# Four tiles for w_in and a new order of batch 0's prologue in a fused cosformer attention and gated MLP kernel

## The chip, the cores and the metric

The kernel runs on one core of a Trainium2 chip. The metric is device time in microseconds (us) of one execution, the median of several. Smaller is better. One further execution is taken by the hardware profiler, and all views of the profile come from it. The engines are called by their short names there: PE (TensorE's products), PEld (its weight loads), DVE (VectorE), ACT (ScalarE), POOL (GpSimd), SP (SyncE, which here only issues loads and stores).

## What is computed

Eight batches, eight heads, 576 positions of 64 numbers each. Linear attention with the feature map phi (a relu times a cosine and a sine of the position, side by side, so 128 features), then a two-layer MLP with x * sigmoid(1.702 x) between.

```python
def phi(x, c, s):
    r = np.maximum(x, 0.0)
    return np.concatenate([r * c, r * s], axis=-1)
q_p = phi(q, cos_w, sin_w)
k_p = phi(k, cos_w, sin_w)
kv = np.einsum('bhsf,bhsd->bhfd', k_p, v)
z = np.sum(k_p, axis=2)
num = np.einsum('bhsf,bhfd->bhsd', q_p, kv)
den = np.einsum('bhsf,bhf->bhs', q_p, z)[..., None] + 1e-06
x = (num / den)                      # then (8, 576, 8 * 64) as 4608 tokens of 512
...
h = x @ w_in                         # 512 x 2048
g = h * (1.0 / (1.0 + np.exp(-1.702 * h)))
return (g @ w_out).astype(np.float32)
```

## The kernel before

The schedule is written out by hand: on each engine the instructions run in the order of the program text, and the framework adds the waits between engines and for loads from what each instruction reads and writes. Matrix operands are bf16, sums are float32 in PSUM. PSUM is used through two pools: `pmm`, four buffers of one bank, and `pat`, two buffers of two banks.

One batch goes through these steps. k and q are loaded as float32 and turned into features by `trig` (line 137), one position block `j` of nine at a time, two instructions each (cosine, sine), on VectorE or, with `act=True`, on ScalarE. One `trig` reads its block for all four pairs of heads. `kv_mm` (L204) multiplies the features of k with v, 36 products of half the array for two pairs of heads; the column of ones beside v gives z. `kv_evac` (L212) copies kv and z to `kvs`. `qturn_pe` (L169) turns two position blocks of q's features with eight transposes on TensorE, and `qevac` (L176) copies them to `qT`. `num_mm` (L218) makes the numerators of one chunk of 128 positions, and in the 65th column of each head the denominators; `num_div` (L226) divides on VectorE: a small add, a reciprocal, and one multiplication of 128x512. `xturn_mm` (L247) transposes the chunk and `xturn_evac` (L254) copies it to x on ScalarE. There are five chunks, the last of 64 positions. `mm1_part` (L271) multiplies x with w_in for one block `fc` of 128 of the 2048 hidden columns, over the four blocks `kc` of the 512; `gelu` (L278) is the activation; `mm2` (L320) multiplies with w_out.

w_in is one tile, `w_in_sb`. `w_in_of(kc, fc)` takes every fourth column of a group of 512, so that `fc // 4` is the group. It is loaded by the Pool queue, which casts to bf16, in three pieces: two groups, then, after a one-element copy that waits for v (`gate`, L133), the other two in one load (L134). A first `gate` (L128) lets v's loads go only after the first piece of k has landed. k and q of batch 0 come by the SP queue, each in two pieces cut along the positions (L61 to L63). Behind w_in the Pool queue issues batch 1's k, two of four w_out groups, batch 1's q and v, and the other w_out groups (L417 to L423), in this order.

Batch 0 has nothing to lie beside, so its prologue is written out at L374 to L414. TensorE is kept busy from the start with products of zeros (`idle`). z of batch 0 is made ahead of v by products with a column of ones, into the same PSUM buffers that later take kv. All of the numerators of chunks 0 and 1 come after both kv groups. Then `start_block` (L345) transposes chunks 0 and 1, makes the numerators of chunk 2, and runs the first four hidden blocks in four pieces of 128 positions, with the numerators and transposes of later chunks between. `mm1(b, 4)` is the first with 512 positions at a time. From there on products follow each other, and the steps of the next batch are placed between them.

Of the kernel before, what the change touches and what calls it, by code (L numbers as in the profile page):

```python
# [9 lines left out]
F32 = mybir.dt.float32  # L10
BF16 = mybir.dt.bfloat16
# [8 lines left out]
def kernel(  # L20
# [39 lines left out]
    qf0 = qf[:, 0:NI * S].rearrange("p (i e) -> p i e", i=NI)  # L60
    for t, src, cut in ((kf, k, 192), (qf0, q, 256)):  # L61
        nc.sync.dma_start(out=t[:, :, 0:cut], in_=src_of(src, 0)[:, :, 0:cut])
        nc.sync.dma_start(out=t[:, :, cut:S], in_=src_of(src, 0)[:, :, cut:S])  # L63


# [32 lines left out]
    qT = one.tile([128, H, 640], BF16, name="qT")  # L98
    w_in_sb = one.tile([128, KC, d_ff], BF16, name="w_in_sb")
    w_out_sb = one.tile([128, FC, d_model], BF16, name="w_out_sb")  # L100
# [5 lines left out]
    wout_r = moe_w_out.rearrange("(g p c) d -> p g c d", p=128, c=4)  # L106
    w_in_v = w_in_sb.rearrange("p k (g f c) -> p k g c f", f=128, c=4)

    def w_in_of(kc, fc):
        return w_in_v[:, kc, fc // 4, fc % 4, :]  # L110

# [8 lines left out]

    def load_win(f0, f1):
        nc.gpsimd.dma_start(out=w_in_sb[:, :, f0:f1], in_=win_r[:, :, f0:f1])  # L122

# [5 lines left out]
    for i in (0, 2):  # L129
        nc.gpsimd.dma_start(out=vb[:, i:i + 2], in_=src_of(v, 0, i, i + 2))  # L130
    load_win(0, 512)
    load_win(512, 1024)
    nc.gpsimd.tensor_copy(gate[0:1, 1:2], vb[0:1, 3, 0:1])  # L133
    load_win(1024, 2048)  # L134

# [59 lines left out]

    def kv_open(i0=0, i1=NI):
        t = pat.tile([128, 2, 512], F32, name="at")
        for i in range(i0, i1):
            st["kv", i] = t[:, :, ds((i - i0) * 65, 65)]
        st["ps", i0] = t[:, :, 0:(i1 - i0) * 65]  # L200
        if i0 == 0:
            st["kvs"] = small.tile([128, 2, NI, VW], BF16, name="kvs", bufs=2)
# [8 lines left out]

    def kv_evac(i0, i1):  # L212
        o = st["kvs"][:, :, i0:i1, 0:65]
        nc.vector.tensor_copy(o, st["ps", i0].rearrange("p hh (i e) -> p hh i e", e=65))  # L214

    nums = {}

    def num_mm(c):  # L218
        ps = pat.tile([128, 2, 512], F32, name="at")
        for h in range(H):  # L220
            i, hh = divmod(h, 2)
            nc.tensor.matmul(ps[:, h // 4, ds((h % 4) * 65, 65)], qT[:, h, ts(c, 128)],  # L222
                             st["kvs"][:, hh, i, 0:65], start=True, stop=True)
        nums[c] = [ps]

    def num_div(c):  # L226
# [43 lines left out]

    def mm1_part(b, fc, t0, t1):  # L271
        if t0 == 0:
            hp[fc] = pmm.tile([128, MT], F32, name="mm")
        for kc in range(KC):
            nc.tensor.matmul(hp[fc][:, t0:t1], w_in_of(kc, fc), x[b][:, kc, t0:t1],  # L275
                             start=(kc == 0), stop=(kc == KC - 1))
# [56 lines left out]

    def idle(n, cols=512):
        w = pmm.tile([128, 512], F32, name="mm")
        for _ in range(n):
            nc.tensor.matmul(w[:, 0:cols], warm[:, 0:128], warm[:, 0:cols], start=True, stop=True)  # L337
# [6 lines left out]

    def start_block(b, opened=False):  # L345

        if not opened:
            xturn_mm(0)
            xturn_evac(b, 0)
            xturn_mm(1)  # L350
            xturn_evac(b, 1)
            num_mm(2)
            num_div(2)
        for c in range(4):
            for fc in range(4):
                mm1_part(b, fc, c * 128, c * 128 + 128)
            if c == 0:
                num_mm(3)
                num_div(3)
                xturn_mm(2)  # L360
                xturn_evac(b, 2)
            if c == 1:
                num_mm(4)
                num_div(4)
                xturn_mm(3)
                xturn_evac(b, 3)
        for fc in range(4):
            gelu(fc)
        mm1(b, 4)
        xturn_mm(4)  # L370
        xturn_evac(b, 4)


    idle(12)  # L374
    idle(100, 64)
    for j in (0, 1):
        trig(kr, kf, j)
    for j in (2, 6, 7, 8):
        trig(kr, kf, j, act=True)
    for j in (3, 4, 5):  # L380
        trig(kr, kf, j)
    kv_open(0, 2)
    kv_open(2, 4)
    kv_mm(0, NI, lambda r, i, j: ones[r, 0:1], 64, 1)
    for j in (0, 1):
        trig(qn0, qf0, j)
    qturn_pe(0)
    for j in (2, 3):
        trig(qn0, qf0, j, act=True)
    qturn_pe(1)  # L390
    idle(3)
    for j in (4, 5):
        trig(qn0, qf0, j)
    qturn_pe(2)
    for j in (6, 7):
        trig(qn0, qf0, j, act=True)
    qevac(0)
    trig(qn0, qf0, 8)
    qevac(1, act=True)
    qevac(2, act=True)  # L400
    kv_mm(0, 2, vb_rhs, 0, 64)
    kv_evac(0, 2)
    kv_mm(2, 4, vb_rhs, 0, 64)
    kv_evac(2, 4)
    qturn_pe(3)
    qevac(3, act=True)
    num_mm(0)
    num_div(0)
    num_mm(1)
    num_div(1)  # L410
    qturn_pe(4)
    qevac(4)
    x_open(0)
    start_block(0)  # L414


# [62 lines left out]
    mm2(0, 3, 12, 16)  # L479
    start_block(1, opened=True)  # L480

# [79 lines left out]
```

## Time and profile before

| | us |
|---|---|
| median of 3 runs | 302.92 (302.34 to 303.1) |
| profiled execution | 303.1 |
| its span, first to last instruction | 301.4 |
| PE busy | 287.0 (95%) |
| PEld busy | 164.4 (55%) |
| DVE busy | 125.9 (42%) |
| ACT busy | 131.4 (44%) |
| POOL busy | 33.9 (11%) |
| mean granted clock of TensorE | 0.989 of full |

In lists of instructions a row has its start and its length in us, the engine, the line, the operation, what it writes and reads, its shape, and how many like it follow (x16); in brackets stands how long the engine was idle before it and what ended that. Rows of loads end with the size in KB and the time from issue to landing. In the chain of waits each piece has its start, its length and what ran. A busy PE is not PE at its peak, since products are pipelined and their ends are modelled.

### The profile page before, as it was taken

The numbers are of one execution on the slowest core, as the hardware profiler recorded it, in microseconds if no ns is written. First come the engines' busy times: TensorE is split into PE (matmuls) and PEld (weight loads), VectorE is DVE, ScalarE is ACT, GpSimd is POOL, SyncE is SP. The second block draws the span as 40 slices with busy tenths as digits, with TensorE's granted clock in tenths as the row PEclk, the third lists the DMA queues.
The fourth block names the chain that finished last, engine by engine and source line by source line (L and its number), as shares of the span: only waits on it lengthen the run. The fifth ranks groups of instructions, "written<-read, shape, count | busy, mean of one in ns | idle before, by whom it ended". The sixth has DMA issues, their size and how long they took to land.

```text
span 301.4 us, 6250 instructions
## 1 busy us (share of the span) xinstructions
PE 287.0 (95%) x2552; PEld 164.4 (55%) x2587; DVE 125.9 (42%) x362; ACT 131.4 (44%) x230; POOL 33.9 (11%) x67
## 2 busy tenths in 40 slices
PE   8829999999999999999999999999999999999995
PEld 4719565685754555455545554555455545565444
DVE  4644802479037444744474447444744430000000
ACT  7822775367311661166116611661166116674111
POOL 6240003240023100100010001000100010000000
PEclk9996999999999999999999999999999999999999
DMA  7999934859536995599549955996599141000331
GB/s 255 235 240 287 344 67 157 310 152 153 159 70 124 362 213 167 107 365 199 179 104 367 193 186 104 366 179 200 102 368 167 54 116 49 3 0 0 80 97 70
DMA packets 66700, 52.38 MB, mean 174 GB/s; under 512 B 47376, under 2 KB 56336, under 8 KB 66672
## 3 DMA queue, kind: packets, MB, share of 16 engines
q1 hardware_dynamic: 59824, 32.52, 42.0%
q0 software_dynamic: 6848, 19.47, 22.4%
q8 instruction: 20, 0.33, 0.4%
q14 instruction: 8, 0.07, 0.1%
HBM read 36.70 MB, written 9.44 MB: 153 GB/s over the span
## 4 chain that ended last, share of the span: by engine, by line
PE 89%; DMA 4%; issue 3%; ACT 1%; POOL 1%; ACTq 0%; POOLq 0%
PE mm L325 41%; PE mm L275 36%; PE mm L293 3%; DMA w_in_sb<-in_moe_w_in_dram 3%; PE at L222 3%; PE at L209 3%; PE mm L302 2%; ACT g L280 1%; DMA kf<-in_k_dram 1%; PE at L252 1%; PE at L173 1%; POOL vb L130 1%; POOL w_in_sb L122 1%; ACT ysb L329 0%; POOL gate L128 0%
## 5 line engine op out<-in xcount | busy, mean ns | idle before, releaser
L275 PE MATMUL mm<-xT,w_in_sb 128*128 128x512 bf16 (+1 forms) x598 | 114.7, 350 | 5.3 <-DMA w_in_sb<-in_moe_w_in_dram 4.9
L325 PE MATMUL mm<-w_out_sb,g 128*128 128x512 bf16 (+1 forms) x506 | 116.3, 373 | 1.3 <-issue 0.2
L275 PEld LDWEIGHTS <-w_in_sb 128*128 128x128 bf16 x608 | 63.6, 115 | 53.9 <-issue 5.0
L280 ACT ACTIVATE g<-mm 128x512 bf16<-128x512 f32 x128 | 75.6, 598 | 32.1 <-PE mm L275 32.1
L325 PEld LDWEIGHTS <-g 128*128 128x128 bf16 x528 | 48.6, 97 | 49.6
L329 ACT ACTIVATE ysb<-mm 128x512 f32<-128x512 f32 (+1 forms) x37 | 21.7, 586 | 111.4 <-PE mm L325 111.4
L332 POOL DMA_DIRECT2D out_dram<-ysb x38 | 20.6, 546 | 177.3 <-ACT ysb L329 177.2
L144 DVE TENSOR_SCALAR kr<-kf,cosw 128x256 bf16<-128x256 f32 x68 | 23.7, 348 | 22.7 <-DMA kf<-in_k_dram 22.7
L234 DVE TENSOR_TENSOR xn<-at,inv 128x512 bf16<-128x512 f32 x40 | 27.6, 691 | 1.6 <-DVE inv L232 0.2
L230 DVE TENSOR_SCALAR den<-at 128x8 f32<-128x8 f32 x40 | 6.6, 166 | 43.9 <-PE at L222 43.9
L144 DVE TENSOR_SCALAR kr<-kf,sinw 128x256 bf16<-128x256 f32 x68 | 23.9, 351 | 0.0
L214 DVE CAST kvs<-at 128x520 bf16<-128x520 f32 (+1 forms) x9 | 5.8, 642 | 33.1 <-PE at L209 33.0
L222 PEld LDWEIGHTS <-qT 128*128 128x128 bf16 x320 | 15.0, 99 | 7.3
L222 PE MATMUL at<-kvs,qT 128*128 128x65 bf16 x320 | 16.4, 196 | 0.0
L157 DVE TENSOR_SCALAR qn<-qf,sinw 128x512 bf16<-128x512 f32 (+1 forms) x30 | 14.3, 477 | 0.0
L157 DVE TENSOR_SCALAR qn<-qf,cosw 128x512 bf16<-128x512 f32 (+1 forms) x30 | 14.3, 476 | 0.0
L209 PEld LDWEIGHTS <-kr 64*128 64x128 bf16 x648 | 10.2, 94 | 3.9 <-issue 3.6
L259 ACT ACTIVATE xT<-at 128x512 bf16<-128x512 bf16 (+1 forms) x10 | 5.6, 563 | 12.2 <-DVE inv L232 9.2
L293 PE MATMUL mm<-xt,w_in_sb 128*128 128x384 bf16 x64 | 10.6, 326 | 0.0
L325 PE MATMUL mm<-w_out_sb,gl_t 128*128 128x512 bf16 x47 | 10.5, 379 | 0.1
L337 PE MATMUL mm<-warm 128*128 128x64 bf16 (+1 forms) x114 | 8.1, 234 | 1.3 <-DVE warm L76 1.3
L293 PEld LDWEIGHTS <-w_in_sb 128*128 128x128 bf16 x64 | 7.2, 113 | 3.3
(60 smaller groups left out, 125.0 us busy)
## 6 DMA issues: line engine op xcount, KB each, us to landing
kf<-in_k_dram SPq DMA_DIRECT2D x5, 1152.0 KB, 6.6
vf<-in_v_dram SPq DMA_DIRECT2D x5, 1152.0 KB, 9.5
qf<-in_q_dram SPq DMA_DIRECT2D x5, 1024.0 KB, 5.5
out_dram<-ysb POOLq DMA_DIRECT2D x20, 256.0 KB, 2.6
kf<-in_k_dram POOLq DMA_DIRECT2D x2, 1152.0 KB, 11.1
vf<-in_v_dram POOLq DMA_DIRECT2D x2, 1152.0 KB, 15.1
out_dram<-ysb POOLq DMA_DIRECT2D x18, 128.0 KB, 3.3
w_out_sb<-in_moe_w_out_dram POOLq DMA_DIRECT2D x4, 512.0 KB, 19.2
```

Source lines behind the costliest of these rows:

```text
L144: nc.vector.tensor_scalar(o, i, 0.0, w[:, j:j + 1], op0=MAX, op1=MUL)
L157: nc.vector.tensor_scalar(o, i, 0.0, sc, op0=MAX, op1=MUL)
L209: nc.tensor.matmul(st["kv", i][:, hh, ds(col, n)], kr[r, j, i, :], rhs(r, i, j), start=(j == 0), stop=(j == NS - 1))
L222: nc.tensor.matmul(ps[:, h // 4, ds((h % 4) * 65, 65)], qT[:, h, ts(c, 128)], st["kvs"][:, hh, i, 0:65], start=True, stop=True)
L234: nc.vector.tensor_tensor(xn, pv[:, :, :, 0:64], inv.unsqueeze(3).to_broadcast([128, 2, 4, 64]), op=MUL)
L275: nc.tensor.matmul(hp[fc][:, t0:t1], w_in_of(kc, fc), x[b][:, kc, t0:t1], start=(kc == 0), stop=(kc == KC - 1))
L280: nc.scalar.activation(g, hp.pop(fc), AF.Gelu_apprx_sigmoid)
L293: nc.tensor.matmul(hps, w_in_of(kc, fc), xt[:, kc, :], start=(kc == 0), stop=(kc == KC - 1))
L325: nc.tensor.matmul(yp[t, c0][:, c0:c1], w, w_out_sb[:, fc, c0:c1], start=(fc == 0), stop=(fc == FC - 1))
L329: nc.scalar.activation(ysb[:, c0:c1], yp[t, c0][:, c0:c1], AF.Identity)
L332: eng.dma_start(out=dst[:, c0:c1], in_=ysb[p0:p0 + n, c0:c1])
L337: nc.tensor.matmul(w[:, 0:cols], warm[:, 0:128], warm[:, 0:cols], start=True, stop=True)
```

## The change

w_in becomes four tiles, one for each group of 512 columns, each with a load of its own. In batch 0's prologue, k is loaded in two pieces cut by pairs of heads and q in one piece, so that each run in memory is whole (576 numbers). z is made by `z_early` in a PSUM buffer of its own and copied to `kvs` at once. The denominators of chunks 0 and 1 are made by `den_mm` (eight products of one column into the buffer of the idle products) and inverted by `den_inv`, `den_mm(w, 0)` ahead of the first kv group, `den_mm(w, 1)` behind it. kv's buffers have 64 columns for each pair, without the one for z. Chunks 0 and 1 are then made by halves of four heads: `num_half`, `div_half`, `turn_half`, `xevac_half`. The q features, turns and evacuations are spread in another order over VectorE and ScalarE, the products of the first two hidden blocks with chunk 0 are split by `kc`, and batch 0's start block is written out with the numerators of chunks 2 to 4 elsewhere. `start_block` is left for batch 1, unchanged there.

```diff
@@ -58,10 +58,9 @@
     qf = one.tile([128, 2560], F32, name="qf")
     kf, vf, vb = raw("kf"), raw("vf"), raw("vb", BF16)
     qf0 = qf[:, 0:NI * S].rearrange("p (i e) -> p i e", i=NI)
-    for t, src, cut in ((kf, k, 192), (qf0, q, 256)):
-        nc.sync.dma_start(out=t[:, :, 0:cut], in_=src_of(src, 0)[:, :, 0:cut])
-        nc.sync.dma_start(out=t[:, :, cut:S], in_=src_of(src, 0)[:, :, cut:S])
-
+    for i in (0, 2):
+        nc.sync.dma_start(out=kf[:, i:i + 2], in_=src_of(k, 0, i, i + 2))
+    nc.sync.dma_start(out=qf0, in_=src_of(q, 0))
 
     NP = NS + 5
     pos_i = const.tile([128, NP], mybir.dt.int32)
@@ -96,7 +95,7 @@
     qn0 = qn.rearrange("p c h f -> p (c h f)")[:, 0:NS * NI * 128].rearrange(
         "p (j i f) -> p j i f", j=NS, i=NI)
     qT = one.tile([128, H, 640], BF16, name="qT")
-    w_in_sb = one.tile([128, KC, d_ff], BF16, name="w_in_sb")
+    w_in_sb = [one.tile([128, KC, 512], BF16, name=f"w_in{g}") for g in range(4)]
     w_out_sb = one.tile([128, FC, d_model], BF16, name="w_out_sb")
     nc.gpsimd.memset(vt[:, :, :, 64:66], 1.0)
     nc.gpsimd.memset(qT[:, :, S:640], 0.0)
@@ -104,10 +103,10 @@
 
     win_r = moe_w_in.rearrange("(kc p) f -> p kc f", p=128)
     wout_r = moe_w_out.rearrange("(g p c) d -> p g c d", p=128, c=4)
-    w_in_v = w_in_sb.rearrange("p k (g f c) -> p k g c f", f=128, c=4)
+    w_in_v = [t.rearrange("p k (f c) -> p k c f", c=4) for t in w_in_sb]
 
     def w_in_of(kc, fc):
-        return w_in_v[:, kc, fc // 4, fc % 4, :]
+        return w_in_v[fc // 4][:, kc, fc % 4, :]
 
     def load(t, src, b, eng=nc.gpsimd):
         eng.dma_start(out=t, in_=src_of(src, b))
@@ -118,8 +117,8 @@
         eng.dma_start(out=qf[0:64, 2048:2560].rearrange("p (h e) -> p h e", h=H),
                             in_=q[b, :, 512:S, :].rearrange("h p d -> p h d"))
 
-    def load_win(f0, f1):
-        nc.gpsimd.dma_start(out=w_in_sb[:, :, f0:f1], in_=win_r[:, :, f0:f1])
+    def load_win(g):
+        nc.gpsimd.dma_start(out=w_in_sb[g], in_=win_r[:, :, ts(g, 512)])
 
     def load_wout(g):
         nc.gpsimd.dma_start(out=w_out_sb[:, ts(g, 4), :], in_=wout_r[:, g])
@@ -128,10 +127,11 @@
     nc.gpsimd.tensor_copy(gate[0:1, 0:1], kf[0:1, 0, 0:1])
     for i in (0, 2):
         nc.gpsimd.dma_start(out=vb[:, i:i + 2], in_=src_of(v, 0, i, i + 2))
-    load_win(0, 512)
-    load_win(512, 1024)
+    load_win(0)
+    load_win(1)
     nc.gpsimd.tensor_copy(gate[0:1, 1:2], vb[0:1, 3, 0:1])
-    load_win(1024, 2048)
+    load_win(2)
+    load_win(3)
 
 
     def trig(dst, src, j, act=False):
@@ -193,12 +193,12 @@
 
     st = {}
 
-    def kv_open(i0=0, i1=NI):
+    def kv_open(i0=0, i1=NI, n=65):
         t = pat.tile([128, 2, 512], F32, name="at")
         for i in range(i0, i1):
-            st["kv", i] = t[:, :, ds((i - i0) * 65, 65)]
-        st["ps", i0] = t[:, :, 0:(i1 - i0) * 65]
-        if i0 == 0:
+            st["kv", i] = t[:, :, ds((i - i0) * n, n)]
+        st["ps", i0] = t[:, :, 0:(i1 - i0) * n]
+        if i0 == 0 and n == 65:
             st["kvs"] = small.tile([128, 2, NI, VW], BF16, name="kvs", bufs=2)
 
     def kv_mm(i0, i1, rhs, col, n):
@@ -209,9 +209,32 @@
                     nc.tensor.matmul(st["kv", i][:, hh, ds(col, n)], kr[r, j, i, :], rhs(r, i, j),
                                      start=(j == 0), stop=(j == NS - 1))
 
-    def kv_evac(i0, i1):
-        o = st["kvs"][:, :, i0:i1, 0:65]
-        nc.vector.tensor_copy(o, st["ps", i0].rearrange("p hh (i e) -> p hh i e", e=65))
+    def kv_evac(i0, i1, n=65):
+        o = st["kvs"][:, :, i0:i1, 0:n]
+        nc.vector.tensor_copy(o, st["ps", i0].rearrange("p hh (i e) -> p hh i e", e=n))
+
+    def z_early():
+        st["kvs"] = small.tile([128, 2, NI, VW], BF16, name="kvs", bufs=2)
+        t = pat.tile([128, 2, 512], F32, name="at")
+        for i in range(NI):
+            for j in range(NS):
+                for hh in range(2):
+                    r = slice(hh * 64, hh * 64 + 64)
+                    nc.tensor.matmul(t[:, hh, i:i + 1], kr[r, j, i, :], ones[r, 0:1],
+                                     start=(j == 0), stop=(j == NS - 1))
+        nc.vector.tensor_copy(st["kvs"][:, :, :, 64], t[:, :, 0:NI])
+
+    def den_mm(dt, c):
+        for h in range(H):
+            i, hh = divmod(h, 2)
+            nc.tensor.matmul(dt[:, ds(c * H + h, 1)], qT[:, h, ts(c, 128)],
+                             st["kvs"][:, hh, i, 64:65], start=True, stop=True)
+
+    def den_inv(dt, c):
+        den = small.tile([128, 2, 4], F32, name="den")
+        nc.vector.tensor_scalar(den, dt[:, ts(c, H)].rearrange("p (a h) -> p a h", a=2), 1e-6, None, op0=ADD)
+        st["inv", c] = small.tile([128, 2, 4], F32, name="inv0", bufs=2)
+        nc.vector.reciprocal(st["inv", c], den)
 
     nums = {}
 
@@ -222,6 +245,31 @@
             nc.tensor.matmul(ps[:, h // 4, ds((h % 4) * 65, 65)], qT[:, h, ts(c, 128)],
                              st["kvs"][:, hh, i, 0:65], start=True, stop=True)
         nums[c] = [ps]
+
+    def num_half(c, a):
+        if a == 0:
+            nums[c] = [pat.tile([128, 2, 512], F32, name="at"),
+                       small.tile([128, 2, 4, 64], BF16, name="xn", bufs=4)]
+        for h in range(4 * a, 4 * a + 4):
+            i, hh = divmod(h, 2)
+            nc.tensor.matmul(nums[c][0][:, a, ds((h % 4) * 65, 64)], qT[:, h, ts(c, 128)],
+                             st["kvs"][:, hh, i, 0:64], start=True, stop=True)
+
+    def div_half(c, a):
+        ps, xn = nums[c]
+        nc.vector.tensor_tensor(xn[:, a], ps[:, a, 0:260].rearrange("p (h e) -> p h e", h=4)[:, :, 0:64],
+                                st["inv", c][:, a].unsqueeze(2).to_broadcast([128, 4, 64]), op=MUL)
+
+    def turn_half(c, a):
+        ps, xn = nums[c]
+        xv = xn[:, a].rearrange("p h e -> p (h e)")
+        for k2 in range(2):
+            nc.tensor.transpose(ps[:, a, ds(264 + k2 * 64, 64)].bitcast(BF16), xv[:, ts(k2, 128)], ident)
+
+    def xevac_half(b, c, a):
+        ps = nums[c][0]
+        i = ps[:, a, 264:392].bitcast(BF16).rearrange("p (k t) -> p k t", k=2)
+        nc.scalar.activation(x[b][:, 2 * a:2 * a + 2, c * 128:c * 128 + 128], i, AF.Copy)
 
     def num_div(c):
         ps = nums[c][0]
@@ -268,10 +316,10 @@
     gT = {}
     hp = {}
 
-    def mm1_part(b, fc, t0, t1):
-        if t0 == 0:
+    def mm1_part(b, fc, t0, t1, k0=0, k1=KC):
+        if t0 == 0 and k0 == 0:
             hp[fc] = pmm.tile([128, MT], F32, name="mm")
-        for kc in range(KC):
+        for kc in range(k0, k1):
             nc.tensor.matmul(hp[fc][:, t0:t1], w_in_of(kc, fc), x[b][:, kc, t0:t1],
                              start=(kc == 0), stop=(kc == KC - 1))
 
@@ -331,8 +379,8 @@
                 eng = nc.sync if b == B - 1 else nc.gpsimd
                 eng.dma_start(out=dst[:, c0:c1], in_=ysb[p0:p0 + n, c0:c1])
 
-    def idle(n, cols=512):
-        w = pmm.tile([128, 512], F32, name="mm")
+    def idle(n, cols=512, w=None):
+        w = pmm.tile([128, 512], F32, name="mm") if w is None else w
         for _ in range(n):
             nc.tensor.matmul(w[:, 0:cols], warm[:, 0:128], warm[:, 0:cols], start=True, stop=True)
 
@@ -342,15 +390,7 @@
     def vt_rhs(r, i, j):
         return vt[r, j, i, 0:65]
 
-    def start_block(b, opened=False):
-
-        if not opened:
-            xturn_mm(0)
-            xturn_evac(b, 0)
-            xturn_mm(1)
-            xturn_evac(b, 1)
-            num_mm(2)
-            num_div(2)
+    def start_block(b):
         for c in range(4):
             for fc in range(4):
                 mm1_part(b, fc, c * 128, c * 128 + 128)
@@ -371,47 +411,88 @@
         xturn_evac(b, 4)
 
 
-    idle(12)
-    idle(100, 64)
-    for j in (0, 1):
+    w = pmm.tile([128, 512], F32, name="mm")
+    idle(12, 512, w)
+    idle(100, 64, w)
+    for j in range(6):
         trig(kr, kf, j)
-    for j in (2, 6, 7, 8):
+    for j in (6, 7, 8):
         trig(kr, kf, j, act=True)
-    for j in (3, 4, 5):
-        trig(kr, kf, j)
-    kv_open(0, 2)
-    kv_open(2, 4)
-    kv_mm(0, NI, lambda r, i, j: ones[r, 0:1], 64, 1)
-    for j in (0, 1):
-        trig(qn0, qf0, j)
+    z_early()
+    trig(qn0, qf0, 0)
+    trig(qn0, qf0, 1, act=True)
+    trig(qn0, qf0, 2)
+    trig(qn0, qf0, 3, act=True)
     qturn_pe(0)
-    for j in (2, 3):
-        trig(qn0, qf0, j, act=True)
+    qevac(0)
+    trig(qn0, qf0, 4)
+    trig(qn0, qf0, 5, act=True)
     qturn_pe(1)
-    idle(3)
-    for j in (4, 5):
-        trig(qn0, qf0, j)
+    qevac(1, act=True)
+    den_mm(w, 0)
+    den_inv(w, 0)
+    kv_open(0, 2, 64)
+    kv_mm(0, 2, vb_rhs, 0, 64)
+    kv_evac(0, 2, 64)
+    den_mm(w, 1)
+    den_inv(w, 1)
     qturn_pe(2)
-    for j in (6, 7):
-        trig(qn0, qf0, j, act=True)
-    qevac(0)
+    qevac(2, act=True)
+    kv_open(2, 4, 64)
+    num_half(0, 0)
+    div_half(0, 0)
+    trig(qn0, qf0, 6)
+    kv_mm(2, 4, vb_rhs, 0, 64)
+    kv_evac(2, 4, 64)
+    turn_half(0, 0)
+    x_open(0)
+    xevac_half(0, 0, 0)
+    num_half(0, 1)
+    div_half(0, 1)
+    num_half(1, 0)
+    div_half(1, 0)
+    trig(qn0, qf0, 7, act=True)
+    num_half(1, 1)
+    div_half(1, 1)
     trig(qn0, qf0, 8)
-    qevac(1, act=True)
-    qevac(2, act=True)
-    kv_mm(0, 2, vb_rhs, 0, 64)
-    kv_evac(0, 2)
-    kv_mm(2, 4, vb_rhs, 0, 64)
-    kv_evac(2, 4)
     qturn_pe(3)
-    qevac(3, act=True)
-    num_mm(0)
-    num_div(0)
-    num_mm(1)
-    num_div(1)
     qturn_pe(4)
+    for fc in (0, 1):
+        mm1_part(0, fc, 0, 128, 0, 2)
+    turn_half(0, 1)
+    xevac_half(0, 0, 1)
+    nums.pop(0)
+    qevac(3)
     qevac(4)
-    x_open(0)
-    start_block(0)
+    turn_half(1, 0)
+    turn_half(1, 1)
+    xevac_half(0, 1, 0)
+    xevac_half(0, 1, 1)
+    nums.pop(1)
+    for fc in (0, 1):
+        mm1_part(0, fc, 0, 128, 2, 4)
+    num_mm(2)
+    num_div(2)
+    for fc in (2, 3):
+        mm1_part(0, fc, 0, 128)
+    num_mm(3)
+    num_div(3)
+    for fc in range(4):
+        mm1_part(0, fc, 128, 256)
+    xturn_mm(2)
+    xturn_evac(0, 2)
+    num_mm(4)
+    num_div(4)
+    xturn_mm(3)
+    xturn_evac(0, 3)
+    for c in (2, 3):
+        for fc in range(4):
+            mm1_part(0, fc, c * 128, c * 128 + 128)
+    for fc in range(4):
+        gelu(fc)
+    mm1(0, 4)
+    xturn_mm(4)
+    xturn_evac(0, 4)
 
 
     load(kf, k, 1)
@@ -477,7 +558,7 @@
     num_mm(2)
     num_div(2)
     mm2(0, 3, 12, 16)
-    start_block(1, opened=True)
+    start_block(1)
 
 
     for b in range(1, B):
```

## The prediction

> **What bounds the kernel now.** I read the page first: TensorE is busy for 95% of a span of 301.4 us, and of the five waits that the list of its waits holds one is long, 4.9 us, for a weight load. Then the chain of waits between 13 and 31 us, and TensorE's instructions in order of time.
>
> ```profile
> 13.35 9.64 DMA w_in_sb<-in_moe_w_in_dram
> ...
> 30.31 0.38 PE mm L275
> ```
> ```profile
> 13.43 1.07 PE L209 MATMUL at<-vb,kr 64*128 64x64 bf16 x60 [1.43 <-issue]
> 14.42 0.62 PE L173 MATMUL mm<-ident,qn 128*128 128x128 bf16 x8
> 14.88 0.66 PE L222 MATMUL at<-kvs,qT 128*128 128x65 bf16 x16
> 15.37 0.39 PE L173 MATMUL mm<-ident,qn 128*128 128x128 bf16 x4
> ...
> 18.03 0.23 PE L275 MATMUL mm<-xT,w_in_sb 128*128 128x128 bf16 x1
> 23.13 1.76 PE L275 MATMUL mm<-xT,w_in_sb 128*128 128x128 bf16 x15 [4.88 <-DMA w_in_sb<-in_moe_w_in_dram]
> ```
>
> The reader should see one product of L275 run at 18.03, and the second wait until 23.13. What it waits for is the third w_in load, issued at 13.35 and landed at 22.99, which brings columns 1024 to 2047; the product needs columns below 512. Of all the data that L275 names, nothing else lands then. So the wait is a false one: with the weights in one tile, its strided slice (every fourth column, `kc` = 1) is taken to overlap the rows that this load writes, while the slice of `kc` = 0 lies below all of them and passed. The stall has a second price, in tables of stages (stage, its length, then busy time of each engine, the granted clock, DMA share, GB/s):
>
> ```profile
> 4.00:6.00 2.00, 2.00 (x23) 1.04 (x22) 1.30 (x4) 0.93 (x3) 1.84 (x4) 1.00 1.07 391
> ...
> 16.00:18.25 2.25, 1.10 (x17) 0.79 (x17) 1.77 (x6) 0.97 (x3) 2.02 (x3) 1.00 1.17 213
> 18.25:23.10 4.85, 0.01 (x1) 0.00 (x0) 1.04 (x3) 0.33 (x1) 0.55 (x1) 0.86 1.10 278
> 23.10:28.30 5.20, 5.17 (x57) 5.20 (x58) 1.38 (x5) 0.60 (x1) 0.00 (x0) 0.50 1.06 268
> ```
>
> After the empty stage TensorE runs for 5.2 us at half clock. The DMA share stays above 1 throughout: the loads go at the rate of the engines, whatever their order.
>
> **What the split of w_in removes.** The first products then need only the first quarter and x. The rows of the loads:
>
> ```profile
> 1.32 0.49 SPq L63 DMA_DIRECT2D kf<-in_k_dram  x1
> 2.40 0.51 SPq L63 DMA_DIRECT2D qf<-in_q_dram  x1
> 4.28 1.63 POOL L130 DMA_DIRECT2D vb<-in_v_dram  x2
> 5.88 1.59 POOL L122 DMA_DIRECT2D w_in_sb<-in_moe_w_in_dram  x2
> ```
> ```profile
> kf<-in_k_dram SPq DMA_DIRECT2D x1, 768.0 KB, 4.7
> qf<-in_q_dram SPq DMA_DIRECT2D x1, 640.0 KB, 7.5
> vb<-in_v_dram POOLq DMA_DIRECT2D x1, 288.0 KB, 8.0
> w_in_sb<-in_moe_w_in_dram POOLq DMA_DIRECT2D x1, 512.0 KB, 9.5
> ```
>
> Issue plus landing: k complete at 6.0, q at 9.9, the second half of v at 5.1 + 8.0 = 13.1, the first quarter of w_in at 15.4. The last is earlier than x (evacuated at 16.95 + 0.60 = 17.6, row below), so the 4.88 us go. The second term is the slow clock. From 23.13 to 30.31 lie 63 products of L275 with 128 columns, 16 of L222 and 8 transposes of L252. At full clock a 128-column product takes 0.058 (eight transposes from 14.42 to 14.88) and one of L222 0.031 (sixteen from 14.88 to 15.37): 71 x 0.058 + 16 x 0.031 = 4.6 us instead of 7.18. Had L275 simply gone on at 18.03, `mm1(0, 4)`, the product at 30.31, would start near 18.03 + 0.06 + 4.6 + 0.1 for a buffer = 22.8: 7.5 us earlier. That is the ceiling.
>
> **What the new prologue gives back.** I walk its order by hand up to the same product. Durations, with start to start where rows follow each other:
>
> ```profile
> 6.07 0.35 DVE L144 TENSOR_SCALAR kr<-kf,cosw 128x256 bf16<-128x256 f32 x1 [0.56 <-DMA kf<-in_k_dram]
> 7.77 0.34 DVE L144 TENSOR_SCALAR kr<-kf,sinw 128x256 bf16<-128x256 f32 x1
> 10.97 0.68 DVE L183 COPY qT<-mm 128x1024 bf16<-128x1024 bf16 x1
> 11.57 0.34 DVE L144 TENSOR_SCALAR qn<-qf,cosw 128x256 bf16<-128x256 f32 x1
> 14.00 0.96 DVE L214 CAST kvs<-at 128x260 bf16<-128x260 f32 x2 [1.82 <-PE at L209]
> 15.33 0.17 DVE L230 TENSOR_SCALAR den<-at 128x8 f32<-128x8 f32 x1 [0.37 <-PE at L222]
> 15.77 0.69 DVE L234 TENSOR_TENSOR xn<-at,inv 128x512 bf16<-128x512 f32 x1
> 28.99 0.34 DVE L144 TENSOR_SCALAR kr<-kf,cosw 128x256 bf16<-128x256 f32 x1
> 33.45 0.34 DVE L144 TENSOR_SCALAR kr<-kf,sinw 128x256 bf16<-128x256 f32 x1
> ```
> ```profile
> 8.48 0.49 ACT L142 ACTIVATE qn<-qf,cosw 128x256 bf16<-128x256 f32 x1
> 11.28 0.49 ACT L142 ACTIVATE qn<-qf,sinw 128x256 bf16<-128x256 f32 x1
> 11.68 1.91 ACT L181 ACTIVATE qT<-mm 128x1024 bf16<-128x1024 bf16 x2
> 16.95 0.60 ACT L259 ACTIVATE xT<-at 128x512 bf16<-128x512 bf16 x1 [0.85 <-PE at L252]
> 32.06 0.43 ACT L259 ACTIVATE xT<-at 128x256 bf16<-128x256 bf16 x1
> ```
>
> A phi on VectorE takes 0.26 (17 steps from 28.99 to 33.45), 0.34 while the Pool queue issues loads (5 steps from 6.07 to 7.77); on ScalarE 0.40 (7 steps from 8.48). A q turn's evacuation takes 0.60 on VectorE, 0.95 on ScalarE; a kv evacuation 0.48; a pair for the denominators 0.44 (15.33 to 15.77). Half a division, 128x256, shows nowhere: between half of 0.69 and all of it; I take 0.35, as 0.69 is nearly all per element. Of products with one column no row is shown: they cost between 0.0165 (half-array products of L209, 60 from 13.43 to 14.42) and 0.031; I take 0.0165 for z, whose weights have the same shape, and 0.031 for the denominators, whose weights are those of L222. A step from one engine to the next I put at 0.15.
>
> k has to be there whole, since each phi reads all of it: the start moves from 4.2 to 6.0. VectorE then does 12 phis, six at 0.34 and six at 0.26: 9.6. Of the 72 z products the first ten go ahead; the others wait for the last phi and end at 10.7. VectorE holds its queue for their copy (0.17 like the row at 15.33), so the first q phi starts at 10.85, later than q's 9.9. From there VectorE's order is nearly gapless: two q blocks to 11.9, evacuation of turn 0 to 12.6, q 4 to 13.1, denominators 13.6, kv of heads 0 to 3 to 14.3 (its products end at 13.8, behind the instruction wait that ended at 13.43 before), denominators 14.75, half division 15.15, q 6 15.7, kv of heads 4 to 7 16.15, three half divisions 17.55, q 8 18.1. ScalarE's share (q 1, 3, 5, 7, turns 1 and 2) lies beside it, and v is early for both kv groups: its gate now waits for 576 KB of k and not 384, 0.2 MB or 0.5 us at 391 GB/s, so its second half lands at 13.6 at worst, and the second group starts at 14.65. TensorE has `qturn_pe(4)` in front of the first products, so these start at 18.35, 0.3 behind the old 18.03.
>
> Behind that: turn 4 0.23, 64 products 3.71, six half-chunk transposes 0.35, 24 number products 0.75, eight transposes 0.46: 5.5 us. Two waits stand in it. The products for `kc` 2 and 3 wait for the second half of chunk 0 (its transposes end at 18.7, its evacuation of 0.43 at 19.3): 0.35. `num_mm(4)` wants the buffer that chunk 2's evacuation of 0.60 frees, and nothing is ahead of it to cover this: 0.77. With 0.4 for semaphores and for the buffer of the first gelu, `mm1(0, 4)` starts at 18.1 + 5.5 + 0.35 + 0.77 + 0.4 = 25.1. **Sum: 30.31 - 25.1 = 5.2 us earlier**, 2.3 short of the ceiling. One more Pool issue (0.8 us) and the wait of batch 1's q load for the last q phi (18.1 instead of 12.2) delay issues behind loads that keep the engines full, so I cost both at nothing. The cover gone, 0.8 would come late where the slack is:
>
> ```profile
> 18.25 0.55 POOL L125 DMA_DIRECT2D w_out_sb<-in_moe_w_out_dram  x1 [0.23 <-DMA w_in_sb<-in_moe_w_in_dram]
> w_out_sb<-in_moe_w_out_dram POOLq DMA_DIRECT2D x1, 512.0 KB, 23.8
> 57.26 1.89 PE L325 MATMUL mm<-w_out_sb,g 128*128 128x512 bf16 x8
> ```
>
> The last load of this stream lands at 42.0, its first reader runs at 57.26, after the change at 52. So the 5.2 us should reach the end. The profiled execution took 303.1 us around its span of 301.4: 303.1 - 5.2 = 297.9. The median shown, 302.92, is 0.2 lower, so I forecast **297.7** for a median. The unknown costs (half divisions up to 0.69 each, column products, semaphores, whole runs landing 0.4 earlier by their longer rows) make it 296.7 to 299.0.
>
> **The rivals.** (a) *Nothing is given back*: k and q land so much earlier in whole runs that the chain hides: 302.9 - 7.5 = 295.4. Against it: the phis of k alone hold VectorE 1.5 us longer than before. 9%. (b) *q comes later*: one long q load shares the engines evenly with v from 5.5 on. Some 1.2 MB of q then take 2.4 MB of traffic, which at 391 GB/s last until 11.6; VectorE's first q phis move by 0.75, ScalarE's by 1.7, turn 0 and all behind it by about 1.1: 298.8. 13%. (c) *The issue of v waits for VectorE's run of phis.* v's second issue, due to start at 5.6, would end with the phis of k at 9.6, land 8.0 later at 17.6, and hold the second kv group from 14.8 to 17.7: +2.9, 300.6. Against it: the two issues beside phis took 1.63, no more than 0.82 each. 5%. [...] (d) *The wait stays*, bound to the load queue and not to the tile: first products again at 23.1, 302.9. Against it: the product at 18.03 passed with the same load in flight. 4%. (e) *The clock falls in the thin prologue* and stays at half for the first 5.2 us of products, as it did from 23.1: 2.6, and TensorE's own pieces of the chain (a q turn 0.46, a denominator group 0.25, a kv group 0.6, number products 0.12) take twice as long, 1.4: 301.7. Against it: 1.10 busy of 2.25 us left it at 1.00, and the longest gap in my walk is about 1 us. 3%. [...] (f) *Slower*: the prologue is now one chain of some 16 steps between engines up to `mm1(0, 4)`, and each costs the 0.85 that ScalarE idled before the evacuation at 16.95, not my 0.15: 16 x 0.7 = 11.2 back, 308.9. It decides from 5.2 / 16 + 0.15 = 0.48 a step. Against it: that 0.85 holds the transposes themselves, and VectorE's 0.37 at 15.33 holds 0.25 of products. 4%.
>
> **How the numbers follow.** The forecast has 62%. A difference under 0.3%, 0.9 us, can't be told from none here. The range from 295.3 to 300.2 holds the forecast, (a) and (b), and leaves (c) to (f) out, 16%, with some of the forecast's tail. Faster: forecast, (a), (b), (c) and most of (e), 0.91; same: (d) and the rest, 0.05; slower: (f), 0.04.
>
> **What would show it.** Right: no wait of L275 for w_in, clock 1.00 throughout 18 to 30 us, the first q phi near 10.85, the first 128-column product near 18.4, the first 512-column product near 25.1, everything later shifted alike. The forecast falls if the first product waits for q, v or a load, if a stage ahead of 25 us shows a clock under 1, or if the distance gained at 25 us shrinks again before the end.

## The result and the profile after

| us | before | after |
|---|---|---|
| median of 13 runs | 302.65 (302.09 to 303.42) | 301.06 (299.11 to 302.07) |
| profiled execution | 303.1 | 300.57 |
| its span | 301.4 | 298.9 |
| mean granted clock in it | 0.989 | 0.983 |

The ratio is 0.9943, 95% interval 0.9923 to 0.9963: faster, by 1.7 us and not by the 5.2 of the forecast. Of the 13 executions after, two took 299.1 us with a mean clock of 0.994, the others 300.6 to 302.1 with 0.977 or 0.983. One execution of `mended` below (310.75 us) fell in a slower state of the chip and is left out of its median and ratio.

The wait for w_in is gone; the list of TensorE's waits no longer names a load. In its place the table by stages of the kernel after (start:end, length, busy time of PE, PEld, DVE, ACT, POOL with counts, granted clock, DMA share, GB/s) shows:

```profile
8.00:10.00 2.00, 1.59 (x69) 1.38 (x67) 1.55 (x6) 0.60 (x3) 0.00 (x0) 1.00 1.14 231
10.00:12.00 2.00, 1.21 (x55) 1.05 (x48) 1.23 (x6) 2.00 (x6) 0.00 (x0) 0.99 1.19 199
12.00:14.00 2.00, 1.96 (x44) 1.59 (x44) 1.51 (x5) 1.36 (x2) 0.57 (x2) 0.50 1.24 204
...
20.00:22.00 2.00, 1.81 (x17) 1.51 (x15) 1.38 (x4) 0.30 (x1) 1.07 (x2) 0.50 1.23 227
22.00:24.00 2.00, 1.96 (x42) 1.87 (x41) 1.11 (x4) 0.74 (x3) 1.55 (x3) 0.94 1.07 403
```

The half clock has not gone, it has moved: it was at 21.7 to 28.6 us and is now at 12.0 to 22.2, over most of the chain that leads to the first products. The chain of waits of the kernel after:

```profile
5.94 3.62 DVE kr L144 x12
9.56 0.04 issue
9.61 0.95 PE at L223 x62
10.58 0.19 DVE kvs L225
10.77 0.51 DVE qn L144 x2
11.28 0.05 issue
11.33 1.48 PE mm L173 x16
...
27.71 0.38 PE mm L323
```

Up to 11.33 it goes as the walk had it (phis from 6.0 to 9.6, z to 10.7, q from 10.85). Then the clock halves. The last row is `mm1(0, 4)`, 2.6 us earlier than before (30.31) and 2.6 later than forecast (25.1). From it to the end of the span are 301.4 - 30.31 = 271.1 us before and 298.9 - 27.71 = 271.2 after: everything behind it only moved, so all of what is missing was lost ahead of it. TensorE's instructions in order of time show the waits there:

```profile
17.70 0.59 PE L255 MATMUL at<-kvs,qT 128*128 128x64 bf16 x8 [0.47 <-ACT xT L272]
19.00 0.38 PE L255 MATMUL at<-kvs,qT 128*128 128x64 bf16 x4 [0.70 <-DVE xn L260]
...
20.82 0.63 PE L323 MATMUL mm<-xT,w_in 128*128 128x128 bf16 x4
...
25.29 0.40 PE L245 MATMUL at<-kvs,qT 128*128 128x65 bf16 x8 [0.69 <-ACT xT L307]
```

L255 is `num_half`. It waits 0.47 for an evacuation by ScalarE and 0.70 for a division by VectorE whose results it does not use: those read the other half of the same two-bank buffer. The wait at 25.29 is that of `num_mm(4)`, forecast at 0.77.

### The profile page after: what moved, and what is told of

It reads as the page before. It is cut to its first block, busy times and chain, and to the rows that moved or that the text cites. A ratio compares the mean times of both kernels' runs of the same rounds, so it can differ in the third digit from the quotient of the medians.

```text
span 298.9 us, 6282 instructions
## 1 busy us (share of the span) xinstructions
PE 288.8 (97%) x2566; PEld 165.4 (55%) x2600; DVE 127.1 (43%) x368; ACT 130.1 (44%) x229; POOL 34.8 (12%) x68
## 4 chain that ended last, share of the span: by engine, by line
PE 92%; DVE 2%; ACT 2%; DMA 2%; issue 1%; SPq 0%; ACTq 0%; DVEq 0%
PE mm L373 41%; PE mm L323 36%; PE at L209 4%; PE mm L341 3%; PE at L245 3%; PE mm L350 2%; DMA kf<-in_k_dram 2%; ACT g L328 1%; DVE kr L144 1%; PE mm L173 1%; PE at L173 1%; PE at L300 1%; DVE qn L144 0%; PE at L255 0%; PE at L223 0%
## 5 line engine op out<-in xcount | busy, mean ns | idle before, releaser
L323 PE MATMUL mm<-xT,w_in 128*128 128x512 bf16 (+1 forms) x598 | 113.3, 345 | 0.5
L323 PEld LDWEIGHTS <-w_in 128*128 128x128 bf16 x608 | 62.3, 114 | 49.2 <-issue 0.2
L377 ACT ACTIVATE ysb<-mm 128x512 f32<-128x512 f32 (+1 forms) x37 | 21.7, 586 | 111.4 <-PE mm L373 111.4
L144 DVE TENSOR_SCALAR kr<-kf,cosw 128x256 bf16<-128x256 f32 x69 | 24.3, 352 | 24.5 <-DMA kf<-in_k_dram 24.5
L282 DVE TENSOR_TENSOR xn<-at,inv 128x512 bf16<-128x512 f32 x38 | 26.3, 691 | 1.3
L245 PEld LDWEIGHTS <-qT 128*128 128x128 bf16 x304 | 14.0, 97 | 8.1 <-issue 0.8
L245 PE MATMUL at<-kvs,qT 128*128 128x65 bf16 x304 | 15.2, 193 | 0.7 <-ACT xT L307 0.7
L341 PE MATMUL mm<-xt,w_in 128*128 128x384 bf16 x64 | 10.6, 326 | 0.0
L341 PEld LDWEIGHTS <-w_in 128*128 128x128 bf16 x64 | 7.2, 113 | 3.3
L342 ACT ACTIVATE gl_t<-mm 128x384 bf16<-128x384 f32 x16 | 7.9, 491 | 2.4 <-PE mm L341 2.4
L165 DVE CAST vt<-vf 128x2304 bf16<-128x2304 f32 (+1 forms) x7 | 8.9, 1266 | 0.0
```

The source lines that it names most:

```text
L144: nc.vector.tensor_scalar(o, i, 0.0, w[:, j:j + 1], op0=MAX, op1=MUL)
L165: nc.vector.tensor_copy(o, i)
L282: nc.vector.tensor_tensor(xn, pv[:, :, :, 0:64], inv.unsqueeze(3).to_broadcast([128, 2, 4, 64]), op=MUL)
L341: nc.tensor.matmul(hps, w_in_of(kc, fc), xt[:, kc, :], start=(kc == 0), stop=(kc == KC - 1))
L377: nc.scalar.activation(ysb[:, c0:c1], yp[t, c0][:, c0:c1], AF.Identity)
```

## The experiments

Each is named by its edit. In the kernels built on the one before, lines stand one further down (L276 for L275).

**The parts alone.** `split_only` is the kernel before with w_in in four tiles; `order_only` is the changed kernel with one tile.

```diff
-    w_in_sb = one.tile([128, KC, d_ff], BF16, name="w_in_sb")
+    w_in_sb = [one.tile([128, KC, 512], BF16, name=f"w_in{g}") for g in range(4)]
...
-    load_win(1024, 2048)
+    load_win(2)
+    load_win(3)
```

> The kernel before with w_in in four tiles and four loads, its prologue and loads of k and q unchanged. Theory A (the reordered prologue is what gives the gain back: the clock falls in it and its halves wait for each other): no wait of the first products for w_in, they go on at 18.0, clock 1.00 up to the first 512-column product, which starts near 22.9 instead of 30.31; 302.65 - 7.4 = 295.2 us, 6 us faster than the changed kernel. Theory B (the changed order is needed, since the old one has x too late or loses the clock in its own gaps once the stall is gone): first 512-column product at 25 or later, 298 to 301 us.

> The changed kernel with w_in in one tile again, its four loads kept. Theory A: the second product of the first hidden block waits for the last load (issued near 14.3, landing near 23.3), so it starts at 23.3 instead of 20.8 and the first 512-column product comes near 30: 303 us, no better than before. If the wait did not belong to the tile, it would show no such wait and 301 us.

`split_only`: 295.86 us, ratio 0.978 (0.9763 to 0.9797). `order_only`: 305.2 us, 1.0085 (1.0067 to 1.0102). So the four tiles by themselves bring 6.7 us, more than the whole change. The new order costs 2.7 where the false wait stays, and 5.2 (301.06 against 295.86) where it is gone. TensorE in `order_only`, in order of time:

```profile
21.38 0.31 PE L323 MATMUL mm<-xT,w_in_sb 128*128 128x128 bf16 x1
24.15 0.48 PE L323 MATMUL mm<-xT,w_in_sb 128*128 128x128 bf16 x3 [2.46 <-DMA w_in_sb<-in_moe_w_in_dram]
```

One product passes and the next waits, as before the change: the wait belongs to the tile. In `split_only` the first products run at 18.78 and the chain has `mm1(0, 4)` here:

```profile
21.92 1.79 PE mm L276 x32
23.73 0.38 PE mm L276
```

That is 4.95 us behind the first product, where the forecast's ceiling had 4.8; the start was 0.75 later than 18.03. By as much the pause of TensorE in the first kv group ended later, at 14.18 instead of 13.43; the products of zeros had ended at 9.7 in this execution, and at 8.5 before.

**The clock.** `after_warm` puts products of zeros into TensorE's gaps around z.

```diff
+    idle(2, 512, w)
     z_early()
+    idle(3, 512, w)
```

> The changed kernel with two 512-column products of zeros ahead of z and three behind it, in TensorE's gaps from 8.8 to 11.3. Theory A1 (the clock fell at 12.0 because between the products of zeros and the first q turn only one-column products run): clock 1.00 from 8 to 28 us in every run, mean clock 0.99, and 299.1 us like the two undisturbed runs of the changed kernel, 2 us less than its median. Rival (the fall costs nothing, since VectorE and the waits between engines set the pace): clock 1.00 but 301 us. Rival (more activity does not hold it): clock 0.5 from 12 us again and 301 us.

298.95 us, ratio 0.9887 (0.9868 to 0.9906), 2.1 us less than after by the medians and 1.7 by the ratios. In three of its four executions the mean clock was 1.0 (298.7 to 299.0 us). The profiled one, 299.97 us, lost it later, at 19.0; its stages:

```profile
12.00:14.00 2.00, 1.46 (x48) 1.08 (x47) 1.47 (x5) 1.80 (x4) 0.52 (x2) 1.00 1.24 204
...
16.00:18.00 2.00, 0.59 (x14) 0.50 (x15) 1.31 (x4) 1.17 (x4) 0.93 (x2) 1.00 1.22 182
18.00:20.00 2.00, 1.40 (x21) 1.23 (x18) 1.76 (x5) 0.00 (x0) 0.34 (x1) 0.74 1.23 204
```

So the fall at 12.0 is prevented by more products there, and it had cost time: that much of theory A1 is shown. "In every run" does not hold: behind the thin stretch at 16 us the clock can fall too. `split_no_idle3` asks whether the three products of zeros between the old q turns, which the change drops, were the cover.

```diff
-    idle(3)
```

> Four w_in tiles in the kernel before, without the three products of zeros between its q turns (512 columns each; the changed kernel leaves them out too). Theory C1 (these products are the cover that the changed order lost): the clock falls near 13 to 15 us and 297 to 298 us come out. Theory C2 (the cover is the 16 q transposes that stand right behind z in the old order and come 0.8 later in the new one): the clock stays at 1.00 and 295.9 us stay.

296.07 us, ratio 0.9784 (0.976 to 0.9808), mean clock 0.998 to 1.00: they were not. What the old order has is q's transposes right behind z; the new order holds them back until VectorE has copied z and made two phis. That these transposes are the cover (theory C2) remains, but is not shown: in `mended` below they follow z at once and the clock falls all the same.

**Whole runs.** `after_cut_loads` has the old pieces of k and q in the changed kernel; `warm_cut` has them with `idle(3, 512, w)` behind z.

```diff
-    for i in (0, 2):
-        nc.sync.dma_start(out=kf[:, i:i + 2], in_=src_of(k, 0, i, i + 2))
-    nc.sync.dma_start(out=qf0, in_=src_of(q, 0))
+    for t, src, cut in ((kf, k, 192), (qf0, q, 256)):
+        nc.sync.dma_start(out=t[:, :, 0:cut], in_=src_of(src, 0)[:, :, 0:cut])
+        nc.sync.dma_start(out=t[:, :, cut:S], in_=src_of(src, 0)[:, :, cut:S])
```

> The changed kernel with k and q of batch 0 loaded in the old pieces, cut by positions. Theory A2 (whole runs cost time because every phi then waits for all of k): the first three phis of k start at 4.2, z ends near 9.7 instead of 10.6, and everything behind moves 0.9 earlier; the gap in TensorE is shorter, so the clock may hold; 298 to 300 us. Rival (whole runs land earlier by their longer rows and this outweighs it): 301 us or more.

> The changed kernel with k and q in the old pieces and three 512-column products of zeros behind z. Theory A2 at full clock: whole runs cost 0.6 us of their own, so with the clock held 298.95 - 0.6 = 298.3 us; the clock stays at 1.00 up to 16 us. Rival: 299 us or more, whole runs cost nothing once the clock is held.

300.45 us (ratio 0.9929, 0.991 to 0.9949) and 299.91 (0.9916, 0.9903 to 0.9929). The first can't be told from the changed kernel. In the second z ended 0.3 us earlier than in `after_warm`, but its kv products resumed at 13.66, against 13.68, and the clock then fell at 19.6 in the profiled execution; all five have a mean clock of 0.994. So what whole runs cost is not shown: something else holds the chain at 13.7.

**The halves.** `warm_order` is `after_warm` with the products of the last three halves together.

```diff
+    num_half(0, 1)
+    num_half(1, 0)
+    num_half(1, 1)
...
     div_half(0, 1)
     turn_half(0, 0)
     xevac_half(0, 0, 0)
     div_half(1, 0)
     trig(qn0, qf0, 7, act=True)
     div_half(1, 1)
```

> The changed kernel with the five products of zeros of after_warm, and the number products of the last three halves issued together, ahead of the transposes and divisions that stood between them. Theory A3 (two halves of one buffer are made to wait for each other's readers: 0.47 for ScalarE's evacuation and 0.70 for VectorE's division in the changed kernel): both waits go, the last q turn starts 0.6 us earlier, 298.3 us against 298.95. Rival (the last q turn waits for VectorE's own work, not for these): no change, 298.9 us.

299.92 us (0.9908, 0.9887 to 0.993), worse: q 7 now stood behind the evacuation on ScalarE, its turn waited 1.04 us, and three of the six executions lost the clock for a while (0.994). `warm_order2` moves `trig(qn0, qf0, 7, act=True)` up behind `num_half(1, 1)`.

> As warm_order, with q 7 ahead of the evacuation on ScalarE, where warm_order had put it behind (its turn then waited 1.04 us for it). Theory A3: neither the two halves' waits nor that one are left, the last q turn starts 0.5 us earlier than in after_warm, 298.4 us. Rival: 298.9 us or more, the halves' waits cover others of the same length.

298.31 us (0.9867, 0.985 to 0.9883). The three groups run as one:

```profile
17.27 0.52 PE L255 MATMUL at<-kvs,qT 128*128 128x64 bf16 x12 [0.74 <-DVE kvs L214]
```

The only wait is for kv, which they need. The gain of 0.64 us over `after_warm` is the size expected, but the two intervals overlap, so it is likely and not certain.

**The hold for z.** `warm_zlate` copies z behind the first q phis, with one product of zeros behind z; `mended` has this, the old pieces, and `warm_order2`'s order, with no products of zeros added.

```diff
-    z_early()
+    zt = z_early()
     trig(qn0, qf0, 0)
...
     trig(qn0, qf0, 3, act=True)
+    nc.vector.tensor_copy(st["kvs"][:, :, :, 64], zt[:, :, 0:NI])
```

> after_warm with the copy of z behind the first two q phis on VectorE in place of ahead of them, and one product of zeros behind z in place of three. Theory A4 (VectorE holds its queue 1.03 us for z although q landed near 9.8): the first q phi starts near 9.9 in place of 10.65, the first q turn 0.3 to 0.5 earlier, 298.5 us. Rival (ScalarE's q 1 is as late): no change, 298.9 us.

> The changed kernel with the old pieces of k and q, the copy of z behind the first q phis, and the number products of three halves ahead, no products of zeros added: the first q turn can follow z at once, as in the kernel before. If clock, whole runs, the hold for z and the halves' waits make up what was given back against split_only, 297 us or less come out, with the clock at 1.00 up to 20 us; what is left to 295.86 is the new order of the start block, whose first 512-column product comes 1.5 to 2 us later behind its first product than the old order's 4.8 us. Rival (the clock falls again, since no large products stand in): 299 us or more.

300.18 us (0.9927, 0.9913 to 0.9942) and 300.54 (0.9931, 0.9912 to 0.995): both miss. The turns came earlier, at 10.68 and 9.96, and nothing came of it. TensorE in `mended`, and its stages:

```profile
11.65 0.41 PE L209 MATMUL at<-vb,kr 64*128 64x64 bf16 x15
13.66 0.74 PE L209 MATMUL at<-vb,kr 64*128 64x64 bf16 x21 [1.61 <-issue]
```
```profile
8.00:10.00 2.00, 2.00 (x109) 1.93 (x106) 1.59 (x7) 2.00 (x7) 0.00 (x0) 1.00 1.17 270
10.00:12.00 2.00, 1.66 (x42) 1.41 (x40) 1.54 (x6) 2.00 (x5) 0.00 (x0) 1.00 1.22 209
12.00:14.00 2.00, 0.39 (x17) 0.33 (x15) 0.16 (x1) 0.14 (x1) 0.47 (x2) 0.59 1.23 204
```

The earlier the first kv group begins, the longer TensorE stops in it for nothing that the profile names: it begins at 12.99 in `after_warm`, 12.69 in `warm_cut`, 12.36 in `warm_zlate` and 11.65 in `mended`, stops for 0.37, 0.63, 1.00 and 1.61 us, and goes on at 13.66 to 13.71 in all four. In `mended` the clock falls within this stop, at 12.4, although TensorE was busy for 3.66 of the 4 us up to 12.0; in `warm_zlate` it falls only at 15.2.

**That stop.** Products of zeros count as two instructions on TensorE, a weight load and a product (L385 in the kernel after: 112 of each), so their number sets at which instruction every later product stands. `split_short_warm` has fewer of them, `split_wide_warm` fewer and larger ones, `split_small_first` the small ones first.

```diff
 split_short_warm, split_only with
-    idle(100, 64)
+    idle(70, 64)
 split_wide_warm, split_only with
-    idle(100, 64)
+    idle(25, 256)
 split_small_first, split_only with
-    idle(12)
-    idle(100, 64)
+    idle(100, 64)
+    idle(9)
```

> Four w_in tiles in the kernel before, with 70 small products of zeros in place of 100. [...]

> Four w_in tiles in the kernel before, with 25 products of zeros of 256 columns in place of 100 of 64, so 150 instructions fewer stand ahead of the kv products on TensorE. [...]

> split_only with the small products of zeros ahead of the large ones (100 of 64 columns, then 9 of 512 in place of 12). In every kernel so far that stopped in this way TensorE stops behind 223 products, 446 instructions. [...] Rival (the wait belongs to v or to the clock): it still ends at 13.4 to 14.2, 295.9 us.

295.69 us (0.9779, 0.9756 to 0.9802), no change that can be told: the first kv group ran without a stop, but the second waited 1.03 us for v, up to 13.42. `split_wide_warm` took 297.27 (0.9808, 0.9782 to 0.9834), so it gained nothing: three executions lost the clock (0.994) and took 297.3 to 297.5, the two that held it 295.9 and 296.0, against 295.86 for `split_only`. But the stop moved, out of kv and into the number products. With it, in order of time, and the instruction queue's one packet between 13.0 and 13.5:

```profile
14.17 0.39 PE L223 MATMUL at<-kvs,qT 128*128 128x65 bf16 x7
15.73 0.43 PE L223 MATMUL at<-kvs,qT 128*128 128x65 bf16 x9 [1.17 <-issue]
```
```profile
q8 instruction: 1, 0.02, 12.2%
```

Counted from the program, the stop stands behind 37 products of zeros, 72 of z, 24 transposes, 72 of kv (with three more of zeros), 8 transposes and 7 number products: 223. In `split_only` it is 112 + 72 + 16 + 3 + 8 + 12 = 223 as well, in the changed kernel 112 + 72 + 16 + 8 + 15 = 223. `split_small_first` took 294.9 us, ratio 0.9754 (0.9737 to 0.9771):

```profile
11.76 0.71 PE L210 MATMUL at<-vb,kr 64*128 64x64 bf16 x36
12.89 0.71 PE L210 MATMUL at<-vb,kr 64*128 64x64 bf16 x36 [0.43 <-DMA vb<-in_v_dram]
```

The stop is gone; the second group waits 0.43 us for v, which it needs. Against `split_only` the intervals overlap a little, and v was there about half a microsecond earlier than in `split_short_warm`, so how much of the 1.0 us is the stop's is not shown. This version beats both kernels of the case, by 7.4 us and 5.7 (by the ratios). The same exchange in `warm_order2` is `warm_small_first`.

> warm_order2 with the same exchange. [...] Rival: the chain is set by VectorE, no change, 298.3 us; or the clock falls without the large products early, 300 us.

297.77 us (0.9844, 0.9829 to 0.9859), 0.54 less than `warm_order2`, though this interval too overlaps that one's: the kv products ran from 13.05 without a stop.

**The start block.** `warm_oldstart` is `warm_order2` with the transposes of chunks 0 and 1, `num_mm(2)`, `num_div(2)` and then the unchanged `start_block(0)` in place of the order written out.

```diff
-    for fc in (0, 1):
-        mm1_part(0, fc, 0, 128, 0, 2)
     turn_half(0, 1)
     xevac_half(0, 0, 1)
...
     num_mm(2)
     num_div(2)
-    for fc in (2, 3):
-        mm1_part(0, fc, 0, 128)
...
+    start_block(0)
```

> warm_order2 with the start block of the kernel before in place of the new one, behind the transposes of both chunks. In warm_order2 the first 512-column product starts 6.6 us behind the first product of L323 (19.49 to 26.09), in split_only 4.95 us (18.78 to 23.73). Theory E (the new order inside the start block, with its waits of 0.68 for chunk 2's evacuation and 0.25 for chunk 0's, costs the rest): those waits go, the distance is 5 us, but the first product starts behind all transposes, near 20.4: 297.6 us against 298.31. Rival: the distance stays above 6 us, 298.3 us or more.

298.2 us (0.9862, 0.983 to 0.9893): no gain in the median, with one of four executions at 0.989 of the clock. In the profiled one the distance from the first product to `mm1(0, 4)` is 19.90 to 24.85, 4.95 us as expected, but the first product starts behind all transposes; from the last q turn it is 6.2 us against 6.8 in `warm_order2`. The wait of 0.68 for chunk 2 is what this saves.

## Why the prediction was wrong

*Right:* the false wait and what it cost. Without it and with the old order `mm1(0, 4)` starts at 23.73, in `split_small_first` at 22.08, against 22.8 for the ceiling. The prologue as far as the first q turn came within 0.2 us of the walk. The shift reached the end undiminished; the later issues on the Pool queue cost nothing.

*The step that failed* is the clock. The walk made all of its sum at full clock and gave rival (e) 3%, because "1.10 busy of 2.25 us left it at 1.00, and the longest gap in my walk is about 1 us". In the profiled execution the clock fell at 12.0 and stayed at half for 10.2 us, although TensorE had been busy for 2.01 of the 3.20 us ahead of that, mostly with z's 72 products of one column. The mean clocks of ten others (0.977 or 0.983) say the same; those of two (0.994) leave room for only a third of that time. So a busy share was no ground to rule the fall out. Five products of 512 columns in the same stretch prevented it there; whether the one-column products let the clock fall, or the 0.8 us of waiting behind them, was not separated. Rival (e) had the right mechanism, but its price of 4.0 us was nearly twice what `after_warm` shows, 2.1. That its 301.7 comes so near to the result is luck: the rest came from two other terms.

*Two smaller terms.* The walk let each half of a chunk run when its own data were there, and put the waits of the halves on one buffer at nothing: 0.64 us by `warm_order2`. The stop of TensorE in the first kv group it took for a fixed time, 13.43, and not for a fixed place in the program: 0.54 us by `warm_small_first`. In the changed kernel itself, at half clock, the stop shows as 0.05 us (13.64 to 13.69 in its chain). Each of these differences is known to about half a microsecond, so the two small ones are likely and not certain. The prediction calls the stop an instruction wait; no run shows what TensorE waits for there, only the place, behind 223 products. Nor does a run show the 0.4 us by which the forecast's range lets whole runs land earlier: all of k was there at 5.8 and not 6.0, q at 9.8 and not 9.9. `warm_small_first` is the changed kernel with all three mended, 297.77 us where 297.7 was forecast, and it passes the places of the walk (a row of TensorE in order of time, then `mm1(0, 4)` in the chain):

```profile
18.34 0.39 PE L323 MATMUL mm<-xT,w_in 128*128 128x128 bf16 x4
```
```profile
24.86 1.02 PE mm L323 x4
```

The walk had the first product at 18.35 and `mm1(0, 4)` at 25.1; VectorE begins its first q phi at 10.70 there (10.85 in the walk) and ends its three half divisions near 17.44 (17.55). So the rest of the walk stands.

*What the new order gives back for good:* `warm_small_first` against `split_small_first`, both without stop and with the clock held in most executions, is 297.77 against 294.9, 2.9 us; the forecast had 2.3. In the profiled ones the first product of w_in comes 1.2 us later (18.34 against 17.14) and `mm1(0, 4)` another 1.6 (24.86 against 22.08): q 6 to 8 and the third q turn now stand behind kv's first group, where the old order had all q features and three of its five turns ahead of it, and the half divisions and their waits are new. Rivals (a) and (d) fell with `split_only` and `order_only`; q was there for ScalarE at 9.83 and not at 11.6, so (b) did not occur, and v's issues took 1.63 us as before, so neither did (c). The steps between engines named "issue" in the chain shown take 0.04 and 0.05 us, less than the 0.15 taken, so (f) did not occur.

*Open:* what exactly makes the clock fall, what whole runs cost by themselves, and how much of the 2.9 us is which of the moved steps.

## What to carry to other kernels

Look whether a product waits for a load that it doesn't read: a strided slice of a tile that several loads fill can be taken to overlap all of them (a wait of 2.46 us in `order_only`), and a tile for each load ends that (no such wait in `split_only`). When a stall is removed or work in a thin prologue is moved, check TensorE's clock along the whole new order, and don't take its busy share for a sign that the clock will hold: 3.66 busy of 4 us in `mended` didn't hold it. Try the parts of a change alone: here one of them was worth four times the whole.

## What the runs showed of the hardware

The granted clock fell to 0.50 at 12.0 us in the changed kernel, 3.2 us behind the last product of zeros (8.8), though PE was 63% busy in between. The stage from there to the fall, in the kernel after:

```profile
8.80:12.00 3.20, 2.01 (x85) 1.68 (x84) 1.98 (x9) 2.17 (x6) 0.00 (x0) 1.00 1.18 201
```

Of its 85 products most are z's, of one column. Five larger products in the same stretch kept the clock up to 19.0 in the profiled execution of `after_warm`. The busy share doesn't decide: 3.66 of 4 us in `mended` were followed by a fall at 12.4, and behind 1.10 of 2.25 us in the kernel before (16.00 to 18.25) it stood at 1.00 through more than 3 us without a product, up to 21.7.

In the falls that the stages show, the half clock lasted a whole number of times 3.41 us. The stages around its two ends in the kernel after:

```profile
11.80:12.00 0.20, 0.20 (x6) 0.15 (x4) 0.01 (x1) 0.20 (x2) 0.00 (x0) 0.95 1.20 199
...
22.20:22.50 0.30, 0.30 (x8) 0.30 (x8) 0.00 (x0) 0.30 (x2) 0.30 (x2) 0.97 1.12 377
```

A mean of 0.95 over 0.20 us is half clock for the last 0.02 us, and 0.97 over 0.30 us for the first 0.02: it lasted from 11.98 to 22.22, 10.24 us. Read in the same way, within about 0.04 us, the half clock lasts 10.24 us in `mended` and `after_cut_loads`, 6.83 in `warm_zlate` and in the kernel before, 3.41 in `after_warm`, `warm_cut`, `warm_order` and `split_wide_warm`, and 17.07 in `order_only`: three, two, one and five times 3.41. In a span of about 299 us one, three and four times 3.41 us make mean clocks of 0.994, 0.983 and 0.977, the values of the 13 executions. The mean of 0.998 in the profiled execution of `split_only`, whose stages from 1 to 30 us all show 1.00, belongs to a stretch that no stage shows: the length is shown for the falls listed alone. In the kernel after, the longest wait of TensorE in the 3.20 us ahead of the fall was 0.79 us.

TensorE stopped behind the same 446th instruction (223 products and their weight loads, counted from the program) in each kernel that stopped, for 0.37 to 1.61 us in the runs listed above (1.43 in the kernel before). One packet of the instruction queue goes by some 2 to 2.7 us before it resumes: between 11.0 and 11.5 in the kernel before (resumed at 13.43), 11.5 and 12 in `split_only` (14.18), 13 and 13.5 in `split_wide_warm` (15.73), and 8.5 and 9 in `split_small_first`, which did not stop. The page's row of that queue (packets, MB, share) for the kernel after:

```profile
q8 instruction: 20, 0.33, 0.4%
```

What TensorE waits for at this place, and whether that packet has to do with it, no run shows.
